# Group normalization in place: 32 written-out tiles become a loop of 8 iterations over 4 fixed buffers

## The chip, the cores and the metric

The kernel runs on one core of a Trainium2 chip. The metric is the device time of one execution in microseconds (us); less is better. The core has five engines that work side by side: TensorE (PE), VectorE (DVE), ScalarE (ACT), GpSimd (POOL) and SyncE (SP). Transfers between memory (HBM) and the on-chip buffers are carried by sixteen DMA engines; an engine such as SP only issues them, in the order of its own instruction stream, and an issue that has to wait on a semaphore holds up everything behind it on that engine.

## The reference

The input `x` is bf16 of shape (128, 1024, 32, 16): 134.2 MB in and as much out. For each of the 128 samples the 1024 channels form 32 groups of 32 channels. Each group is normalized with its own mean and variance, then scaled and shifted by channel:

```python
    xr = x.reshape(B, G, C // G, H, W)
    mu = xr.mean(axis=(2, 3, 4), keepdims=True)
    var = ((xr - mu) ** 2).mean(axis=(2, 3, 4), keepdims=True)
    xn = (xr - mu) / jnp.sqrt(var + 1e-5)
    xn = xn.reshape(B, C, H, W)
    return xn * g[None, :, None, None] + b[None, :, None, None]
```

## The kernel before

One tile holds 4 samples: the 128 partitions are 4 samples by 32 groups, and each partition holds one group of 32 channels by 512 positions, 16,384 bf16 values. A tile is 4 MB, loaded with one DMA and stored with one DMA, and there are `NT` = 32 of them. A tile is normalized in place: the store reads the buffer that the load filled.

Work on a tile `i`, in order:

- `sums` (line 130): PE adds up the tile, 32 matmuls of 512 columns with an identity matrix, accumulated in one PSUM tile `ps`.
- `squares` (lines 148 and 161): ACT takes a rough shift `nshift` from the first 512 values, then sums the squares of the shifted values in four parts of 4096.
- `moments` (lines 180 to 213): DVE reduces `ps` to the negative mean, and with the shift and the four sums of squares gets the variance (`jv`, line 213).
- `root` (line 231): ACT takes the square root. `apply` (lines 241 to 264): DVE takes the reciprocal, forms scale and offset by channel (`scl`, `bia`), and applies them with 32 instructions of 512 values each.
- `store(i)` (line 78), and then `load(i + 5)` (line 74) into the buffer of tile `i - 1`. Both are issued by SP.

The loop over the tiles is a Python loop, so the program is written out: all 32 tiles stand one behind the other in each engine's instruction stream. The helper `chain` fixes the order of each engine's instructions as they are written. `XBUFS` = 6 buffers are loaded ahead of the loop. The scale and the offset (`g` and `b`, 2 KB each, needed by all four samples) are fetched with eight small DMAs issued by ACT. DMAs share eight completion semaphores in turn; one that takes a semaphore again waits until its former DMA has landed.

Of the kernel before, what the change touches and what calls it, by code (L numbers as in the profile page):

```python
# [10 lines left out]
F32 = mybir.dt.float32  # L11
BF16 = mybir.dt.bfloat16
# [1 line left out]
NUM_GROUPS = 32  # L14
EPS = 1e-5

XBUFS = 6
MM_FREE = 512
SQ_PARTS = 4

# [2 lines left out]
def kernel(  # L23
# [8 lines left out]
    nc = tc.nc  # L32
    P = nc.NUM_PARTITIONS
    B0, C, H, W = x.shape
    G = NUM_GROUPS
# [3 lines left out]
    NT = B0 // NS  # L39
    F = KC * HW  # L40
# [4 lines left out]
    x_v = x.rearrange("(t n) (q k) h w -> t (n q) (k h w)", n=NS, q=G)  # L45
    o_v = out.rearrange("(t n) (q k) h w -> t (n q) (k h w)", n=NS, q=G)
    g_v = g.rearrange("(q k) -> q k", q=G)
    b_v = b.rearrange("(q k) -> q k", q=G)

    consts = ctx.enter_context(tc.tile_pool(name="consts", bufs=1))  # L50
    xpool = ctx.enter_context(tc.tile_pool(name="xpool", bufs=XBUFS))
    jpool = ctx.enter_context(tc.tile_pool(name="jpool", bufs=1))
    spool = ctx.enter_context(tc.tile_pool(name="spool", bufs=4))
    pspool = ctx.enter_context(
        tc.tile_pool(name="pspool", bufs=3, space=bass.MemoryType.PSUM)
    )

    last = {}
# [4 lines left out]
    def chain(key, inst):  # L63
        prev = last.get(key)
        if prev is not None:
            tc.add_manual_dep(inst.ins, prev.ins.name, nosync, reason="engine order")
        last[key] = inst
        return inst

    state = {}  # L70

    def load(i):
        xt = xpool.tile([P, F], BF16, name="xt")
        chain("sp", nc.sync.dma_start(out=xt[:], in_=x_v[i]))  # L74
        state[i] = {"xt": xt}

    def store(i):
        chain("sp", nc.sync.dma_start(out=o_v[i], in_=state[i]["xt"][:]))
        state.pop(i)

    for i in range(XBUFS):
        load(i)

    gam_b = consts.tile([P, KC], BF16)
    bet_b = consts.tile([P, KC], BF16)
    for n in range(NS):
        chain("act", nc.scalar.dma_start(out=gam_b[n * G : (n + 1) * G, :], in_=g_v))
        chain("act", nc.scalar.dma_start(out=bet_b[n * G : (n + 1) * G, :], in_=b_v))

    eps_t = consts.tile([P, 1], F32)  # L90
    nc.vector.memset(eps_t[:], EPS)  # L91
# [7 lines left out]
        out=half[:],  # L99
        in_=ones[:],  # L100
# [6 lines left out]
    eye = consts.tile([P, P], BF16)  # L107
    nc.gpsimd.affine_select(  # L108
        out=eye[:],
        in_=half[:],  # L110
# [9 lines left out]
    chain("dve", nc.vector.tensor_copy(out=gam[:], in_=gam_b[:]))  # L120
    chain("dve", nc.vector.tensor_copy(out=bet[:], in_=bet_b[:]))

    def sums(i):

        st = state[i]
        ps = pspool.tile([P, MM_FREE], F32, name="ps")
        for k in range(NMM):
            chain(
                "pe",
                nc.tensor.matmul(  # L130
                    out=ps[:],
                    lhsT=eye[:],
                    rhs=st["xt"][:, k * MM_FREE : (k + 1) * MM_FREE],
                    start=(k == 0),
                    stop=(k == NMM - 1),
                ),
            )
        st["ps"] = ps

    def squares(i):  # L140

        st = state[i]
        xt = st["xt"]
        nshift = spool.tile([P, 1], F32, name="nshift")
        ja = jpool.tile([P, SQ], BF16, name="ja")
        chain(
            "act",
            nc.scalar.activation(  # L148
                out=ja[:, 0:HW],
                in_=xt[:, 0:HW],  # L150
                func=ACT.Identity,
                scale=-1.0 / HW,
                accum_out=nshift[:],
            ),
        )
        sq = spool.tile([P, SQ_PARTS], F32, name="sq")
        for k in range(SQ_PARTS):
            ja = jpool.tile([P, SQ], BF16, name="ja")
            chain(
                "act",  # L160
                nc.scalar.activation(  # L161
                    out=ja[:],
                    in_=xt[:, k * SQ : (k + 1) * SQ],
                    func=ACT.Square,
                    bias=nshift[:],
                    scale=1.0,
                    accum_out=sq[:, k : k + 1],
                ),
            )
        st["nshift"] = nshift  # L170
        st["sq"] = sq

    def moments(i):

        st = state[i]
        negmean = spool.tile([P, 1], F32, name="negmean")
        jd = jpool.tile([P, MM_FREE], BF16, name="jd")
        chain(
            "dve",
            nc.vector.tensor_scalar(  # L180
                out=jd[:],
                in0=st["ps"][:],
                scalar1=-inv_n,
                scalar2=None,
                op0=ALU.mult,
                op1=ALU.add,
                accum_out=negmean[:],
            ),
        )
        d = spool.tile([P, 1], F32, name="d")  # L190
        chain(
            "dve",
            nc.vector.tensor_tensor(  # L193
                out=d[:], in0=negmean[:], in1=st["nshift"][:], op=ALU.subtract
            ),
        )
        nd2 = spool.tile([P, 1], F32, name="nd2")
        chain(
            "dve",
            nc.vector.tensor_scalar(  # L200
                out=nd2[:],
                in0=d[:],
                scalar1=d[:],
                scalar2=-1.0,
                op0=ALU.mult,
                op1=ALU.mult,
            ),
        )
        var = spool.tile([P, 1], F32, name="var")
        jv = spool.tile([P, SQ_PARTS], F32, name="jv")  # L210
        chain(
            "dve",
            nc.vector.tensor_scalar(  # L213
                out=jv[:],
                in0=st["sq"][:],
                scalar1=inv_n,
                scalar2=nd2[:],
                op0=ALU.mult,
                op1=ALU.add,
                accum_out=var[:],  # L220
            ),
        )
        st["negmean"] = negmean
        st["var"] = var

    def root(i):
        st = state[i]
        rstd = spool.tile([P, 1], F32, name="rstd")
        chain(
            "act",  # L230
            nc.scalar.activation(  # L231
                out=rstd[:], in_=st["var"][:], func=ACT.Sqrt, bias=eps_t[:], scale=1.0
            ),
        )
        st["rstd"] = rstd

    def apply(i):
        st = state[i]
        rstd = st["rstd"]
        xt = st["xt"]  # L240
        chain("dve", nc.vector.reciprocal(out=rstd[:], in_=rstd[:]))  # L241
        scl = spool.tile([P, KC], F32, name="scl")
        bia = spool.tile([P, KC], F32, name="bia")
        chain(
            "dve",
            nc.vector.tensor_scalar(  # L246
                out=scl[:], in0=gam[:], scalar1=rstd[:], scalar2=None, op0=ALU.mult
            ),
        )
        chain(  # L250
            "dve",
            nc.vector.scalar_tensor_tensor(  # L252
                out=bia[:],
                in0=scl[:],
                scalar=st["negmean"][:],
                in1=bet[:],
                op0=ALU.mult,
                op1=ALU.add,
            ),
        )  # L260
        for k in range(KC):
            chain(
                "dve",
                nc.vector.tensor_scalar(  # L264
                    out=xt[:, k * HW : (k + 1) * HW],
                    in0=xt[:, k * HW : (k + 1) * HW],
                    scalar1=scl[:, k : k + 1],
                    scalar2=bia[:, k : k + 1],
                    op0=ALU.mult,
                    op1=ALU.add,  # L270
                ),
            )

    for i in range(NT):
        sums(i)
        squares(i)
        moments(i)
        root(i)
        apply(i)
        store(i)  # L280
        if i >= 1 and i + XBUFS - 1 < NT:
            load(i + XBUFS - 1)


# [28 lines left out]
```

## Time and profile before

| | |
|---|---|
| Median of 3 runs | 639.44 us (638.84 to 639.48) |
| Time of the profiled execution | 638.97 us |
| Its span in the profile | 637.3 us |
| DMA | 268.71 MB, mean 422 GB/s; the load and store queue q1 takes 98.2% of 16 engines' span |
| Busy share of the span | ACT 82%, DVE 62%, PE 45% |
| One tile on ACT | 4 x 3708 ns of squares, 624 ns for the shift, 5 x about 186 ns of accumulator reads, 294 ns for the root |
| One tile of `apply` on DVE | 32 x 404 ns mean, starts about 0.33 us apart: 10.4 us |

The profiled execution's time is 1.67 us more than its span, which runs from the first to the last instruction. The page cuts the span into 40 slices of 15.9 us; a digit is a busy share in tenths, and 9 means 90% or more. In the chain of work that ended last each piece has its start, its length and what it was; a DMA's piece runs from its issue to its landing, so the time that it spends queued behind older transfers is part of it. In a list of waits each line names who waited, for whom, the total, the number of times and the longest wait; "SPq" is SP's issuing queue.

### The profile page before, as it was taken

Reading aid. Unit: us, or ns where it says so; the run is one execution under the profiler, and the core shown is the slowest. Engines: PE = TensorE matmul, PEld = TensorE weight load, DVE = VectorE, ACT = ScalarE, POOL = GpSimd, SP = SyncE. Lnnn points to the kernel's source line nnn. Section 1 sums busy time; section 2 is a strip of 40 time slices with the busy share of each in tenths; the row PEclk is TensorE's granted clock in tenths of the full one; section 3 lists DMA queues with packets and bytes.
Section 4 is the critical chain, followed back from the end, with each engine's and each line's share of the span. In section 5 each row is a group of like instructions: output and inputs, shape, how many; then the busy total and the mean of one; then the engine's idle time right before and its main releaser. Section 6 shows DMA issues by size and latency. Waiting matters only on the chain.

```text
span 637.3 us, 3988 instructions
## 1 busy us (share of the span) xinstructions
PE 289.4 (45%) x1004; PEld 113.9 (18%) x1024; DVE 395.7 (62%) x1316; ACT 519.5 (82%) x354; POOL 0.8 (0%) x6
## 2 busy tenths in 40 slices
PE   1868505544355542556334654335652356533400
PEld 0323202211122211222111221112220122211100
DVE  0277777777777755577655676555765557755560
ACT  2999999999999887988788978879887898788800
POOL 0000000000000000000000000000000000000000
PEclk9899857656877567876678766787666877667755
DMA  7999999999999999999999999999999999999993
GB/s 301 438 436 403 430 437 433 428 430 428 430 438 430 434 426 432 427 440 426 436 434 431 428 438 432 432 427 438 430 429 435 435 430 432 430 432 433 436 430 171
DMA packets 9623, 268.71 MB, mean 422 GB/s; under 512 B 1408, under 2 KB 1408, under 8 KB 1408
## 3 DMA queue, kind: packets, MB, share of 16 engines
q1 hardware_dynamic: 9216, 268.44, 98.2%
q8 instruction: 8, 0.13, 0.1%
q14 instruction: 15, 0.12, 0.0%
q10 hardware_dynamic: 384, 0.02, 0.0%
HBM read 134.23 MB, written 134.22 MB: 421 GB/s over the span
## 4 chain that ended last, share of the span: by engine, by line
DMA 73%; ACT 13%; PE 6%; DVE 4%; issue 0%; SPq 0%; DVEq 0%; ACTq 0%
DMA out_dram<-xt 48%; DMA xt<-in_x_dram 25%; ACT ja L161 12%; PE ps L130 6%; DVE xt L264 3%; ACT ja L148 1%; DVE jd L180 0%; SPq L74 0%; DVE jv L213 0%; ACT rstd L231 0%; DVE bia L252 0%; DVE scl L246 0%; DVE rstd L241 0%; DVEq L308 0%; DVE nd L200 0%
## 5 line engine op out<-in xcount | busy, mean ns | idle before, releaser
L161 ACT ACTIVATE ja<-xt,nshift 128x4096 bf16<-128x4096 bf16 x128 | 474.6, 3708 | 4.1
L130 PE MATMUL ps<-xt,eye 128*128 128x512 bf16 x1004 | 289.4, 455 | 307.5 <-DMA xt<-in_x_dram 281.2
L264 DVE TENSOR_SCALAR xt<-xt,scl,bia 128x512 bf16<-128x512 bf16 x1024 | 333.6, 404 | 1.2
L130 PEld LDWEIGHTS <-eye 128*128 128x128 bf16 x1024 | 113.9, 114 | 482.5 <-DMA xt<-in_x_dram 303.0
L213 DVE TENSOR_SCALAR_CACHE_REDUCE jv<-sq,nd 128x4 f32<-128x4 f32 x32 | 6.9, 217 | 157.4 <-ACT ja L161 157.4
L148 ACT ACTIVATE ja<-xt 128x512 bf16<-128x512 bf16 x32 | 20.0, 624 | 63.8 <-DMA xt<-in_x_dram 63.8
L180 DVE TENSOR_SCALAR_CACHE_REDUCE jd<-ps 128x512 bf16<-128x512 f32 x32 | 22.0, 688 | 28.8 <-PE ps L130 27.3
L161 ACT ACTIVATION_READ_ACCUMULATOR ja<-xt,nshift 128x1 f32 x128 | 23.9, 186 | 0.0
L231 ACT ACTIVATE rstd<-var,eps_t 128x1 f32<-128x1 f32 x32 | 9.4, 294 | 9.4 <-DVE jv L213 9.4
L241 DVE RECIPROCAL rstd<-rstd 128x1 f32<-128x1 f32 x32 | 5.2, 164 | 11.6 <-ACT rstd L231 11.6
L252 DVE SCALAR_TENSOR_TENSOR bia<-scl,negmean,bet 128x32 f32<-128x32 f32 x32 | 8.0, 251 | 1.1
L246 DVE TENSOR_SCALAR scl<-gam,rstd 128x32 f32<-128x32 f32 x32 | 7.7, 242 | 1.1
L120 DVE CAST gam<-gam_b 128x32 f32<-128x32 bf16 x1 | 0.2, 181 | 12.9 <-DMA bet_b<-in_b_dram 12.9
L200 DVE TENSOR_SCALAR nd<-d 128x1 f32<-128x1 f32 x32 | 6.9, 214 | 1.1
L93 ACT ACT_TABLE_LOAD x1 | 1.3, 1283 | 7.3 <-DMA gam_b<-in_g_dram 7.3
L193 DVE TENSOR_TENSOR d<-negmean,nshift 128x1 f32<-128x1 f32 x32 | 5.1, 159 | 3.3
L148 ACT ACTIVATION_READ_ACCUMULATOR ja<-xt 128x1 f32 x32 | 6.0, 187 | 0.0
L213 DVE DVE_READ_ACCUMULATOR jv<-sq,nd 128x1 f32 x32 | 2.6, 83 | 0.0
L180 DVE DVE_READ_ACCUMULATOR jd<-ps 128x1 f32 x32 | 2.6, 82 | 0.0
L91 DVE MEMSET eps_t<- 128x1 f32 x1 | 0.1, 59 | 0.9 <-PEq L297 0.9
L98 POOL TENSOR_SCALAR_AFFINE_SELECT half<-ones 128x128 bf16<-128x128 bf16 x1 | 0.3, 295 | 0.7 <-DVE ones L96 0.7
L108 POOL TENSOR_SCALAR_AFFINE_SELECT eye<-half 128x128 bf16<-128x128 bf16 x1 | 0.3, 294 | 0.1
(7 smaller groups left out, 0.9 us busy)
## 6 DMA issues: line engine op xcount, KB each, us to landing
xt<-in_x_dram SPq DMA_DIRECT2D x32, 4096.0 KB, 29.0
out_dram<-xt SPq DMA_DIRECT2D x32, 4096.0 KB, 39.1
gam_b<-in_g_dram ACTq DMA_DIRECT2D x4, 2.0 KB, 10.3
bet_b<-in_b_dram ACTq DMA_DIRECT2D x4, 2.0 KB, 9.8
```

Of the source, the lines that this page charges most:

```text
L130: nc.tensor.matmul(out=ps[:], lhsT=eye[:], rhs=st["xt"][:, k * MM_FREE : (k + 1) * MM_FREE], start=(k == 0), stop=(k == NMM - 1),),
L148: nc.scalar.activation(out=ja[:, 0:HW], in_=xt[:, 0:HW], func=ACT.Identity, scale=-1.0 / HW, accum_out=nshift[:],),
L161: nc.scalar.activation(out=ja[:], in_=xt[:, k * SQ : (k + 1) * SQ], func=ACT.Square, bias=nshift[:], scale=1.0, accum_out=sq[:, k : k + 1],),
L180: nc.vector.tensor_scalar(out=jd[:], in0=st["ps"][:], scalar1=-inv_n, scalar2=None, op0=ALU.mult, op1=ALU.add, accum_out=negmean[:],),
L193: nc.vector.tensor_tensor(out=d[:], in0=negmean[:], in1=st["nshift"][:], op=ALU.subtract),
L200: nc.vector.tensor_scalar(out=nd2[:], in0=d[:], scalar1=d[:], scalar2=-1.0, op0=ALU.mult, op1=ALU.mult,),
L213: nc.vector.tensor_scalar(out=jv[:], in0=st["sq"][:], scalar1=inv_n, scalar2=nd2[:], op0=ALU.mult, op1=ALU.add, accum_out=var[:],),
L231: nc.scalar.activation(out=rstd[:], in_=st["var"][:], func=ACT.Sqrt, bias=eps_t[:], scale=1.0),
L241: chain("dve", nc.vector.reciprocal(out=rstd[:], in_=rstd[:]))
L246: nc.vector.tensor_scalar(out=scl[:], in0=gam[:], scalar1=rstd[:], scalar2=None, op0=ALU.mult),
L252: nc.vector.scalar_tensor_tensor(out=bia[:], in0=scl[:], scalar=st["negmean"][:], in1=bet[:], op0=ALU.mult, op1=ALU.add,),
L264: nc.vector.tensor_scalar(out=xt[:, k * HW : (k + 1) * HW], in0=xt[:, k * HW : (k + 1) * HW], scalar1=scl[:, k : k + 1], scalar2=bia[:, k ...
```

## The change

The 32 tiles become a hardware loop of 8 iterations, each of which works through 4 tiles. The buffers are four fixed tiles `x0` to `x3`. Across iterations, waits compare semaphores with registers that grow from one iteration to the next (`iteration_sync="reg_based"`). The addresses of loads and stores come from the loop variable. Three loads stand ahead of the loop, not six; in the loop, tile `i` is followed by `store(i)` and the load of tile `i + 3`. In the last iteration the loads past the end carry a condition that skips them. Stores are declared not to depend on each other. The scale and offset loads move from ACT to SP, between loads 0 and 1. Each tile gets two small new instructions, a one-column matmul into `pt` on PE and a one-column copy into `jt` on ACT, which read the tile before the large ones do.

```diff
-XBUFS = 6
+XBUFS = 4
...
-    xpool = ctx.enter_context(tc.tile_pool(name="xpool", bufs=XBUFS))
+    xpool = ctx.enter_context(tc.tile_pool(name="xpool", bufs=1))
...
+    ptpool = ctx.enter_context(
+        tc.tile_pool(name="ptpool", bufs=1, space=bass.MemoryType.PSUM)
     )
...
-    def load(i):
-        xt = xpool.tile([P, F], BF16, name="xt")
-        chain("sp", nc.sync.dma_start(out=xt[:], in_=x_v[i]))
-        state[i] = {"xt": xt}
-
-    def store(i):
-        chain("sp", nc.sync.dma_start(out=o_v[i], in_=state[i]["xt"][:]))
-        state.pop(i)
-
-    for i in range(XBUFS):
-        load(i)
+    bufs = [xpool.tile([P, F], BF16, name=f"x{j}") for j in range(XBUFS)]
+
+    def load(j, i, cond=None):
+        chain("sp", nc.sync.dma_start(out=bufs[j][:], in_=x_v[i], cond=cond))
+
+    def store(j, i):
+
+        st = chain("sp", nc.sync.dma_start(out=o_v[i], in_=bufs[j][:]))
+        tc.declare_no_dep(st.ins, group="stores", across_iterations=True, reason="rows of its own")
+        tc.add_to_no_dep_group("stores", st.ins)
+
+    load(0, 0)
...
-        chain("act", nc.scalar.dma_start(out=gam_b[n * G : (n + 1) * G, :], in_=g_v))
-        chain("act", nc.scalar.dma_start(out=bet_b[n * G : (n + 1) * G, :], in_=b_v))
+        chain("sp", nc.sync.dma_start(out=gam_b[n * G : (n + 1) * G, :], in_=g_v))
+        chain("sp", nc.sync.dma_start(out=bet_b[n * G : (n + 1) * G, :], in_=b_v))
+
+    for j in range(1, XBUFS - 1):
+        load(j, j)
...
+        pt = ptpool.tile([P, 1], F32, name="pt")
+        chain(
+            "pe",
+            nc.tensor.matmul(
+                out=pt[:], lhsT=eye[:], rhs=st["xt"][:, 0:1], start=True, stop=True
+            ),
+        )
...
+        jt = jpool.tile([P, 1], BF16, name="jt")
+        chain("act", nc.scalar.copy(out=jt[:], in_=xt[:, 0:1]))
...
-    for i in range(NT):
-        sums(i)
-        squares(i)
-        moments(i)
-        root(i)
-        apply(i)
-        store(i)
-        if i >= 1 and i + XBUFS - 1 < NT:
-            load(i + XBUFS - 1)
+    def compute(j):
+        st = {"xt": bufs[j]}
+        sums(st)
+        squares(st)
+        moments(st)
+        root(st)
+        apply(st)
+
+    with tc.For_i(0, NT, XBUFS, iteration_sync="reg_based") as t:
+        last.clear()
+        for j in range(XBUFS):
+            compute(j)
+            store(j, t + j)
+            n = XBUFS - 1 + j
+            load(n % XBUFS, t + n if j == 0 else (t + n) % NT, None if j == 0 else t < NT - XBUFS)
```

More of the change, by code (lines that the diff above doesn't have):

```diff
@@ L68, in chain @@
         return inst
-    state = {}
-    def load(i):
-        xt = xpool.tile([P, F], BF16, name="xt")
-        chain("sp", nc.sync.dma_start(out=xt[:], in_=x_v[i]))
-        state[i] = {"xt": xt}
-    def store(i):
-        chain("sp", nc.sync.dma_start(out=o_v[i], in_=state[i]["xt"][:]))
-        state.pop(i)
-    for i in range(XBUFS):
-        load(i)
+    bufs = [xpool.tile([P, F], BF16, name=f"x{j}") for j in range(XBUFS)]
[6 more added lines that the diff above has]
+    load(0, 0)
     gam_b = consts.tile([P, KC], BF16)
@@ L121, with sums @@
     chain("dve", nc.vector.tensor_copy(out=bet[:], in_=bet_b[:]))
-    def sums(i):
-        st = state[i]
+    def sums(st):
+        pt = ptpool.tile([P, 1], F32, name="pt")
[4 more added lines that the diff above has]
+            ),
+        )
         ps = pspool.tile([P, MM_FREE], F32, name="ps")
@@ L138, in sums, with squares @@
         st["ps"] = ps
-    def squares(i):
-        st = state[i]
+    def squares(st):
         xt = st["xt"]
+        jt = jpool.tile([P, 1], BF16, name="jt")
+        chain("act", nc.scalar.copy(out=jt[:], in_=xt[:, 0:1]))
         nshift = spool.tile([P, 1], F32, name="nshift")
@@ L171, in squares, with moments @@
         st["sq"] = sq
-    def moments(i):
-        st = state[i]
+    def moments(st):
         negmean = spool.tile([P, 1], F32, name="negmean")
@@ L224, in moments, with root @@
         st["var"] = var
-    def root(i):
-        st = state[i]
+    def root(st):
         rstd = spool.tile([P, 1], F32, name="rstd")
@@ L235, in root, with apply @@
         st["rstd"] = rstd
-    def apply(i):
-        st = state[i]
+    def apply(st):
         rstd = st["rstd"]
```

## The prediction

> **What bounds the kernel now.** I began with the engine totals and the 40 slices of the page.
>
> ```profile
> PE 289.4 (45%) x1004; PEld 113.9 (18%) x1024; DVE 395.7 (62%) x1316; ACT 519.5 (82%) x354; POOL 0.8 (0%) x6
> ...
> DMA  7999999999999999999999999999999999999993
> GB/s 301 438 436 403 430 437 433 428 430 428 430 438 430 434 426 432 427 440 426 436 434 431 428 438 432 432 427 438 430 429 435 435 430 432 430 432 433 436 430 171
> ```
>
> No compute engine is full (ACT leads with 82%), but the DMA row reads 9 from the second slice to the last but one. The sixteen DMA engines set the time, and only the first and last slices show them short of work. Next, the chain that ended last, where it stands on transfers.
>
> ```profile
> 0.80 12.25 DMA xt<-in_x_dram
> ...
> 126.36 38.82 DMA out_dram<-xt
> ...
> 165.64 39.23 DMA out_dram<-xt
> ...
> 519.18 39.09 DMA out_dram<-xt
> ...
> 558.35 28.97 DMA xt<-in_x_dram
> ```
>
> A load into an idle queue takes 12.25 us (the first; it lands at 13.05). In the stream a store takes 39 us because three transfers stand before it. The store issued at 126.36 is tile 5's and lands at 165.18; the one issued at 519.18 is tile 25's and lands at 558.27. So 20 tiles take 393.09 us: **19.65 us for one load and one store**, 9.83 us each. The last load lands at 587.32. Then SP's timeline and its waits.
>
> ```profile
> 40.97 0.35 SPq L78 DMA_DIRECT2D out_dram<-xt  x1
> ```
>
> ```profile
> 615.29 0.33 SPq L78 DMA_DIRECT2D out_dram<-xt  x1
> ```
>
> ```profile
> SPq L74 <- DMA out_dram<-xt: 472.4, 26, 19.5
> SPq L78 <- DVE xt L264: 100.1, 7, 25.4
> SPq L74 <- DMA xt<-in_x_dram: 11.9, 1, 11.9
> ```
>
> Tile 0's store goes out at 40.97, 27.92 us after its load landed; the last at 615.29, 27.97 us after its own. That 28 us is the **tile latency**: ACT's squares, the moments, then 32 DVE applications. SP's 26 long waits are loads that wait until an older store has emptied a buffer; the wait of 11.9 us shows that already now the second load goes out only after the first has landed. The DMA view of the last 23 us gives the last store's time:
>
> ```profile
> out_dram<-xt SPq DMA_DIRECT2D x1, 4096.0 KB, 21.1
> ```
>
> It lands at 636.4, and 0.9 us later the span ends (637.3). It was issued 21 us ahead, so it still queued behind older stores: neither the first nor the last tile's latency is exposed today.
>
> **The change, part by part.** *Scale and offset loads on SP.* Eight issues stand on SP between loads 0 and 1, and in the built program the last of them waits for load 0, as load 1 does now. Seven issues at about 0.45 us (from ACT's timeline, 0.42 to 0.69) fit in the 11.9 us that SP waits there; the eighth puts loads 1 and 2 0.5 us later, nothing to the end, since ACT reaches tile 1 only 16.5 us after tile 0. ACT loses its eight issues and its 7.3 us before the table load, worth nothing: it waits for load 0 anyway.
>
> *Three loads ahead instead of six, and load 3 behind store 0.* This decides the start. In SP's new order load 3 stands behind store 0, although its buffer is empty, and store 0 waits for the tile latency. Tile latency grows by ACT's touch copy (128x1; the rows of that size on ACT are 0.20 and 0.29 us) and some register instructions, unshown; the 0.02 us pieces between instructions on the chain bound them at some 0.1 us together, one 0.4 us DMA issue from above. I take 0.3: 28.3 us. Load 2 lands at 13.05 + 0.5 + 12.3 + 9.7 = 35.6 and the queue runs dry. Store 0 goes out at 13.05 + 28.3 = 41.4 and, from an idle queue, lands 12.3 us later: 53.7. An idle store is not in the trace; 12.25 is the idle load's row, and 9.7 (no start-up at all) and 15 bound it. The order is then load 3, store 1, load 4, ..., so tile 4's store is the twelfth transfer and lands at 53.7 + 8 x 9.83 = 132.3. The twelfth transfer before is tile 3's store, which the chain lands at 125.9. **Start: +6.4 us.**
>
> *The middle.* A tile's store follows its load in the queue after four others (39.3 us). It needs the tile latency (28.3) and must be issued 2.6 us early (12.3 - 9.7): 8.4 us to spare. ACT needs 16.5 us a tile beside 19.65. Each load waits for the store before last, as now, and goes out as that lands, two transfers ahead of its turn. So four buffers still keep the queue full; the copy, PE's extra 1-column matmul (at most 0.46 + 0.11 us; PE idles 10 us a tile) and register waits lie under the 8.4 us. Dynamic addresses may add a fraction of a 0.4 us issue on SP, hidden by its long waits. A late back edge is hidden too: behind a waiting SP stand the next store and load, and both have this reserve. I take **0** for the seven back edges; bounds are -0.3 us a tile (clean pairs at 19.36, from neighbouring loads' landings; say -8 in all) and +2 us an iteration (+14).
>
> *The end.* Load 31 lands last among the loads, after store 28, as transfer 61: 53.7 + 57 x 9.83 = 614.0. Only stores 29 and 30 follow, 19.7 us of work, and then the queue is dry until store 31 goes out at 614.0 + 28.3 = 642.3, landing 12.3 later at 654.6. Before, transfer 61 landed three transfers before 636.4, near 607.2. So after transfer 61 it now takes 40.6 us, not 29.2: **end +11.4 us**. Three loads are skipped; their waits (the store before last) stand on SP ahead of stores 30 and 31, but stores 28 and 29 land before the data of 30 and 31 are ready. Loop exit adds a barrier: 0.5 taken, 0 to 3 us. The span ends at 654.6 + 0.9 + 0.5 = **656.0**.
>
> The sum is against the profiled execution: span 637.3, time 638.97, thus 1.67 outside the span; the median of the three runs is 0.47 higher. 656.0 + 1.67 + 0.47 = 658.1.
>
> The Trainium skill, in DMA: Bandwidth & Descriptors, section Anatomy of one DMA, gives a transfer as 2.0 us plus its bytes over 436 GB/s. By it an idle 4 MB transfer would be estimated at 11.6 us, not 12.25, and the sum 1.3 us lower. I keep the row.
>
> **The rivals.** *Back edges cost the stream.* The unrolled program fetches its instructions in order:
>
> ```profile
> q8 instruction: 8, 0.13, 0.1%
> q14 instruction: 15, 0.12, 0.0%
> ```
>
> That is 8 fetches of 16 KB and 15 of 8 KB. The loop could refetch its body each time (DVE's is 205 instructions, PE's 277), and either stall an engine or take DMA time. The q8 row's 0.1% of 16 engines' span is some 10 us, about 1.3 us a fetch; two more such on one DMA engine per iteration give 2 to 3 us x 7, near 672. For it: one late DMA engine holds up every landing. Against: an engine's stall has 8.4 us of cover, and ACT's 2.7 us idle a tile absorbs it. The Trainium skill, Runtime: NRT & Kernel Launch, section Instruction fetch mechanics, speaks for this rival: prefetch is sequential and a taken branch out of a two-page window stalls for a fetch. By that rule each engine would stop at each back edge, and by its 16 KB pages a DVE body of 205 could stay inside; the trace's second queue shows 8 KB pieces, not 16. No run here yet shows a back edge.
>
> *Four buffers are too few.* If latency plus issue exceeds 39.3 us, every tile pays. With 2 us over, 28 x 2 = 56: near 714; 0.5 us over, near 672. It needs 8.4 us that I can't name.
>
> *The waits don't overlap iterations.* If growing registers act as a drain, each of seven back edges exposes about 40.6 - 29.5 + 6.4 = 17.5 us: near 781. The waits in the built program compare with counts that the previous iteration has reached long before, so this is weak. So is the skip that does not skip: three loads, +10 us to +29.
>
> *A cleaner stream* (a small form of the next): landings 9.68 us apart without the fetches between, -8: 650.
>
> *Other side: a stream fast enough to pay for both ends.* Fewer transfers in flight and fewer fetches could speed up the pairs. Price: 28 pairs x the gain; it decides from 18.7 / 28 = 0.67 us a pair, that is 18.98 us, or 442 GB/s. Then 639.4, and less beyond. For it: some slices reach 438 to 440. Against: no full slice passes 440, and the clean pairs stop at 19.36.
>
> **How the numbers follow.** Forecast, both ends exposed and a full stream: 0.62. Cleaner stream, 650: 0.14. Back edges, 672: 0.12. Too few buffers: 0.05. Drains or unskipped loads: 0.04. Other side: 0.03, of it 0.01 within the 0.2% that a measurement of this kernel can tell from no change. The predicted time is the likeliest case's, 658. The range is 647 to 672: from the cleaner stream with a quick idle store (2.5 us less) to the back edges. Faster 0.02, same 0.01, slower 0.97.
>
> **What would show it.** Right: the DMA row falls in the third slice (near 36 to 44 us) and again near the end; the first store issues near 41 and lands near 54; steady pairs 19.65 us apart; the last load lands near 614 and the last store, issued 28 us later, takes about 12 us instead of 21. Wrong: pairs further apart or dips at every fourth tile (back edges), no dip at the start (load 3 got ahead of store 0), or a store issued late against its turn in the middle.

## The result, and the profile after

The changed kernel takes 663.53 us (median of 4 runs, 663.13 to 664.49) and the kernel before 639.27 us beside it (638.84 to 639.48): a ratio of 1.0383, 95% interval 1.0365 to 1.0401. The change costs some 24 us; 19 were predicted. The profiled execution took 663.21 us with a span of 661.2.

The page of the changed kernel: busy time of the engines, the DMA engines' share in 40 slices (16.5 us each), and the two queues.

```profile
PE 293.0 (44%) x1040; PEld 116.2 (18%) x1056; DVE 396.4 (60%) x1316; ACT 523.5 (79%) x386; POOL 0.8 (0%) x6
...
DMA  7949999999999999999999999999999999999555
GB/s 288 442 191 381 444 420 434 438 426 428 434 430 430 430 426 434 432 422 440 436 422 440 434 424 438 436 424 440 432 418 436 420 416 422 434 424 430 230 256 254
...
q1 hardware_dynamic: 9600, 268.46, 95.2%
q14 instruction: 2, 0.02, 0.0%
```

The compute engines do the same work as before. The two places where the DMA row falls are the two of the prediction: the third slice (4; 191 GB/s) and now the last three (5 5 5). Between them it is all 9: the loop leaves no dip at any fourth tile. The row of the 16 KB instruction fetches (q8) is gone, and q14 holds 2 fetches where the written-out kernel had 15.

SP's timeline at the start and at the end (start, length, instruction):

```profile
13.23 0.31 SPq L91 DMA_DIRECT2D bet_b<-in_b_dram  x1
13.58 0.91 SPq L77 DMA_DIRECT2D x<-in_x_dram  x2
...
43.09 0.36 SPq L81 DMA_DIRECT2D out_dram<-x  x1
43.80 0.36 SPq L77 DMA_DIRECT2D x<-in_x_dram  x1
...
628.37 0.36 SPq L81 DMA_DIRECT2D out_dram<-x  x1
...
647.91 0.36 SPq L81 DMA_DIRECT2D out_dram<-x  x1
648.78 0.08 SPq L77 DMA_DIRECT2D x<-in_x_dram  x1
```

Load 3 stands behind store 0, and nothing is issued between 14.5 and 43.1 us while loads 1 and 2 land at 25.88 and 35.59: the queue is dry for 7.5 us. At the end a skipped load costs SP 0.08 us, and store 31 goes out into an idle queue.

The chain that ended last, in order of time; a DMA's piece runs from issue to landing:

```profile
0.81 12.40 DMA x<-in_x_dram
13.23 1.48 DMA bet_b<-in_b_dram
...
331.60 21.62 DMA out_dram<-x
...
568.83 21.62 DMA out_dram<-x
590.60 29.31 DMA x<-in_x_dram
```

A store now lands 21.6 us after its issue, not 39: fewer transfers stand before it. Tile 15's store lands at 353.22 and tile 27's at 590.45, so 12 tiles take 237.23 us, **19.77 us a tile** (19.65 before). The last load lands at 619.91, 28.0 us before store 31 goes out. The second piece was not expected on this chain: a load of 2 KB stands between load 0 and the first work on it.

The prediction's points against the trace, with the written-out twin of the first experiment in the last column (us from the start of the span):

| | before | predicted | after | twin |
|---|---|---|---|---|
| tile 0 starts on ACT | 13.08 | 13.1 | 14.95 | 13.13 |
| store 0 issued | 40.97 | 41.4 | 43.09 | 41.12 |
| store 0 lands (after its issue) | 76.67 | 53.7 (12.3) | 55.18 (12.1) | 53.22 (12.1) |
| steady pairs | 19.65 | 19.65 | 19.77 | 19.65 |
| load 31 lands | 587.3 | 614.0 | 619.9 | 616.1 |
| store 31 issued | 615.3 | 642.3 | 647.9 | 644.1 |
| store 31 lands (after its issue) | 636.4 (21.1) | 654.6 (12.3) | 659.0 (11.1) | 655.2 (11.1) |
| span ends | 637.3 | 656.0 | 661.2 | 656.0 |

### The profile page after: what moved, and what is told of

Read it like the earlier page. It is cut to its first block, busy times and chain, and to the rows that moved or that the text cites. A ratio compares the mean times of both kernels' runs of the same rounds, so it can differ in the third digit from the quotient of the medians.

```text
span 661.2 us, 5054 instructions
## 1 busy us (share of the span) xinstructions
PE 293.0 (44%) x1040; PEld 116.2 (18%) x1056; DVE 396.4 (60%) x1316; ACT 523.5 (79%) x386; POOL 0.8 (0%) x6
## 3 DMA queue, kind: packets, MB, share of 16 engines
q1 hardware_dynamic: 9600, 268.46, 95.2%
## 4 chain that ended last, share of the span: by engine, by line
DMA 59%; issue 23%; DVE 13%; ACT 2%; DVEq 0%; SPq 0%; ACTq 0%
DMA x<-in_x_dram 36%; DMA out_dram<-x 23%; DVE x L274 12%; ACT ja L174 1%; ACT ja L161 0%; ACT rstd L242 0%; DVE bia L262 0%; DVE scl L256 0%; DMA bet_b<-in_b_dram 0%; DVE rstd L251 0%; DVE jv L225 0%; ACT jt L156 0%; DVEq L292 0%; SPq L77 0%; DVEq L324 0%
## 5 line engine op out<-in xcount | busy, mean ns | idle before, releaser
L174 ACT ACTIVATE ja<-x,nshift 128x4096 bf16<-128x4096 bf16 x128 | 474.6, 3708 | 4.1
L274 DVE TENSOR_SCALAR x<-x,scl,bia 128x512 bf16<-128x512 bf16 x1024 | 333.6, 405 | 2.1
L142 PE MATMUL ps<-x,eye 128*128 128x512 bf16 x1008 | 290.5, 456 | 2.2 <-issue 1.8
L134 PE MATMUL pt<-x,eye 128*128 128x1 bf16 x32 | 5.5, 173 | 334.4 <-DMA x<-in_x_dram 246.7
L142 PEld LDWEIGHTS <-eye 128*128 128x128 bf16 x1024 | 114.2, 114 | 168.0 <-issue 92.7
L156 ACT COPY jt<-x 128x1 bf16<-128x1 bf16 x32 | 6.2, 193 | 98.9 <-DMA x<-in_x_dram 83.4
L134 PEld LDWEIGHTS <-eye 128*128 128x128 bf16 x32 | 3.3, 104 | 344.9 <-DMA x<-in_x_dram 153.5
L174 ACT ACTIVATION_READ_ACCUMULATOR ja<-x,nshift 128x1 f32 x128 | 23.8, 186 | 0.0
L161 ACT ACTIVATE ja<-x 128x512 bf16<-128x512 bf16 x32 | 20.1, 628 | 0.0
L251 DVE RECIPROCAL rstd<-rstd 128x1 f32<-128x1 f32 x32 | 5.2, 164 | 11.6 <-ACT rstd L242 11.6
L161 ACT ACTIVATION_READ_ACCUMULATOR ja<-x 128x1 f32 x32 | 6.0, 186 | 0.0
```

The source lines that it names most:

```text
L134: nc.tensor.matmul(out=pt[:], lhsT=eye[:], rhs=st["xt"][:, 0:1], start=True, stop=True),
L142: nc.tensor.matmul(out=ps[:], lhsT=eye[:], rhs=st["xt"][:, k * MM_FREE : (k + 1) * MM_FREE], start=(k == 0), stop=(k == NMM - 1),),
L156: chain("act", nc.scalar.copy(out=jt[:], in_=xt[:, 0:1]))
L161: nc.scalar.activation(out=ja[:, 0:HW], in_=xt[:, 0:HW], func=ACT.Identity, scale=-1.0 / HW, accum_out=nshift[:],),
L174: nc.scalar.activation(out=ja[:], in_=xt[:, k * SQ : (k + 1) * SQ], func=ACT.Square, bias=nshift[:], scale=1.0, accum_out=sq[:, k : k + 1],),
L274: nc.vector.tensor_scalar(out=xt[:, k * HW : (k + 1) * HW], in0=xt[:, k * HW : (k + 1) * HW], scalar1=scl[:, k : k + 1], scalar2=bia[:, k ...
```

## The experiments

The theory after the first result: both ends cost what the prediction says, and the 5 us more come from the loop itself, at its entry, through the small loads, and at its exit. Its rivals: the loop slows the transfers in the middle (register addresses, conditions, back edges), or the four buffers do; then a written-out kernel of the same order would be at the predicted 658 only by accident.

### Is it the loop, or the order and the four buffers?

**twin_unrolled**: the changed kernel's order, buffers and small instructions, written out.

```diff
-    with tc.For_i(0, NT, XBUFS, iteration_sync="reg_based") as t:
...
+    for i in range(NT):
+        compute(i % XBUFS)
+        store(i % XBUFS, i)
+        n = i + XBUFS - 1
+        if n < NT:
+            load(n % XBUFS, n)
```

> The changed kernel written out: four fixed buffers, three loads ahead, store i then load i+3, parameter loads on SP, touch instructions, but a Python loop instead of the hardware loop. Theory 1 (the order of the transfers costs, not the loop): near the changed kernel, 660 to 664 us, with the same dry queue near 36 to 43 us and the last store issued about 28 us after the last load lands. Within it, two small terms of the loop should move: tile 0 starts near 13.2 us instead of 14.9, because no engine waits for another to enter a loop (-1.7 us), and load-store pairs are 19.65 us as in the kernel before (instruction fetches come back) or stay 19.77 (then it is the four buffers). Theory 2 (the back edges and register waits cost): at or below 645 us.

Measured: 658.18 us (657.73 to 658.55), ratio 1.0301 [1.0284, 1.0318], span 656.0, somewhat below the expected times. So about 19 us come from order and depth, and the loop itself costs 5.3 us. The table's last two columns say where: 2.0 at store 0, 1.8 in the stream, 1.4 between the last landing and the end of the span (2.2 against 0.8). The page of the twin has both dips without any loop:

```profile
DMA  7959999999999999999999999999999999999665
```

That the twin's span is the predicted 656.0 to the tenth is luck: its stream from store 0 to load 31 is 2.6 us longer than the sum had it (562.9, not 560.3), and its other terms are 2.6 us shorter together.

**before_4_buffers**: the kernel before with `XBUFS` = 4 (not 6); its own order keeps load 3 ahead of store 0.

> The kernel before with 4 buffers instead of 6: written out, its own order and parameter loads, four loads ahead. Theory 1: both ends are exposed, a little less at the start than in the changed kernel: 652 to 656 us, last store issued 28 us after the last load landed and taking 11 to 12 us instead of 21. Rival (four buffers are enough, the loop costs): 639 to 641 us.

Measured: 654.58 us (654.47 to 654.72), 1.0243 [1.0226, 1.026], as expected. Its steady pairs are 19.67: four buffers keep the queue full in the middle. The cost is at the ends: its last load lands at 612.87, and nothing covers the last tile. From its chain that ended last:

```profile
583.89 28.98 DMA xt<-in_x_dram
```

The three runs take the change apart: of the 24 us, some 15.5 come with four buffers, another 3.6 with the rest of the twin (load 3 behind store 0, the small loads on SP, the small instructions), and 5.3 with the loop.

**before_5_buffers**: the same with `XBUFS` = 5.

> The kernel before with 5 buffers instead of 6. With 4 it took 654.6. Theory 1 (the ends are exposed only where less than the tile latency of 28 us is queued behind the last load): the last load is then followed by three other stores (29 us) before the last one, just enough, and five loads (51 us) cover the first 41 us: 639 to 640 us, no different from 6 buffers. Rival (each buffer less costs its share): half of the way to 4 buffers, 646 to 647.

Measured: 639.49 us (638.98 to 640.22), 1.0007 [0.9997, 1.0016]: no difference from six. Each buffer less moves the last load later (587.3, 598.2, 612.9), and one tile of 28.0 us and one idle store of 11.1, 39.1 us together, are a floor under the end behind it. With four buffers the last store lands on that floor (651.93). With five the floor is at 637.3, and the last store lands at 637.67, 9.65 us behind the one before it, as in a full stream; the stream of the six-buffer kernel runs out at 636.43. Five is where the floor meets the stream.

### Load 3 behind store 0

**loop_load3_ahead**: load 3 goes ahead of the loop, and its place in the first iteration is skipped.

```diff
-    for j in range(1, XBUFS - 1):
+    for j in range(1, XBUFS):
...
-            load(n % XBUFS, t + n if j == 0 else (t + n) % NT, None if j == 0 else t < NT - XBUFS)
+            load(n % XBUFS, t + n if j == 0 else (t + n) % NT, t > 0 if j == 0 else t < NT - XBUFS)
```

> The changed kernel with load 3 put ahead of the loop (and skipped in the first iteration), so that it no longer stands behind store 0. Theory 1: the dry queue before store 0 is filled by load 3, but a shorter one opens behind store 0, since load 4 stands behind store 1, which waits for tile 1 (issue near 59.7): in all 3 us less, 660 to 661 us. Rival (the start is hidden work, only the end costs): no change, 663.5. Rival (the whole gap of the start is load 3's place): 7 us less, 656.5.

Measured: 660.67 us (659.84 to 661.24), 1.0335 [1.0318, 1.0352], 2.9 us less than the changed kernel and as expected. The dip gets shallower (247 GB/s in its lowest early slice, not 191) and the last load lands at 617.65, not 619.91. It does not vanish: the queue is now dry behind store 0, which lands at 55.56, until store 1 goes out at 60.11, and load 4 stands behind that store.

### The 1.9 us at which tile 0 starts later

The profile of the changed kernel names the loop's own line (292) as what tile 0 waits for. From its list of waits (who, for whom: total, times, longest):

```profile
DVE gam L126 <- DMA gam_b<-in_g_dram: 13.4, 1, 13.4
ACT jt L156 <- SPq L292: 12.6, 1, 12.6
```

At the entry to the loop PE, ACT, SP and DVE each signal the others (PE and ACT by 1.0 us, SP and DVE only from 14.5 to 15.1), and the first reads of load 0, on PE and ACT, wait for SP's and DVE's signals. DVE enters only after its two casts; these wait for the eight small loads. Seven of them, issued from 1.26 to 4.12 us, land only behind load 0, from 13.38 to 14.40; the eighth, which takes over load 0's completion semaphore, is issued at 13.23 and lands at 14.71. The timeline shows them in line:

```profile
14.52 0.18 DVE L126 CAST gam<-gam_b 128x32 f32<-128x32 bf16 x1 [13.40 <-DMA gam_b<-in_g_dram]
14.73 0.18 DVE L127 CAST bet<-bet_b 128x32 f32<-128x32 bf16 x1
14.95 0.19 ACT L156 COPY jt<-x 128x1 bf16<-128x1 bf16 x1 [12.64 <-SPq L292]
```

In the twin ACT does not wait for the casts:

```profile
13.13 0.19 ACT L156 COPY jt<-x 128x1 bf16<-128x1 bf16 x1 [10.83 <-DMA x<-in_x_dram]
14.39 0.18 DVE L126 CAST gam<-gam_b 128x32 f32<-128x32 bf16 x1 [13.29 <-DMA gam_b<-in_g_dram]
```

Two experiments moved the eight loads, in the loop kernel, to **loop_params_act** and **loop_params_pool**:

```diff
-        chain("sp", nc.sync.dma_start(out=gam_b[n * G : (n + 1) * G, :], in_=g_v))
+        chain("act", nc.scalar.dma_start(out=gam_b[n * G : (n + 1) * G, :], in_=g_v))
```

(the second with `chain("pool", nc.gpsimd.dma_start(...))`; both move the `bet_b` loads likewise).

> The changed kernel with the scale and offset loads back on ACT. The loop starts an engine's work on tile 0 only when SP and DVE have set the semaphores that they own at the loop's entry. Theory 1a (DVE's entry holds tile 0): the last small load still waits for load 0, DVE still casts after it, tile 0 still starts near 14.9: 663 to 664 us, although loads 1 and 2 go out near 7 us instead of 13.6. Theory 1b (only SP's eight issues hold tile 0): SP enters early, tile 0 starts near 13.2, 661.5 to 662 us.

Measured: 663.32 us (663.05 to 664.58), 1.0389 [1.0372, 1.0406]: no gain. Loads 1 and 2 go out at 13.23 and 13.62, not near 7 as expected; SP still enters the loop some 0.4 us earlier. But the last small load, though issued at 7.06, lands at 14.31, again behind load 0, and ACT's wait is now put down to DVE:

```profile
14.68 0.19 ACT L156 COPY jt<-x 128x1 bf16<-128x1 bf16 x1 [5.78 <-DVEq L292]
```

> The changed kernel with the scale and offset loads on GpSimd's queue, so that neither SP nor DVE waits for load 0 ahead of the loop. Theory 1 (a or b): tile 0 starts near 13.2 us instead of 14.9 and store 0 goes out near 41.3 instead of 43.1: 661.5 to 662 us. Rival (tile 0's late start comes from the loop's branch and first fetch, not from the small loads): 663.5.

Measured: 672.89 us (672.38 to 673.51), 1.0529 [1.0512, 1.0547]: 9.4 us slower than the changed kernel where a gain was expected. It shows the mechanism by its opposite. With nothing between loads 0 and 1, SP issues all three large loads by 2.2 us; the small loads on GpSimd then share the sixteen engines with 12 MB, and land one after the other from 8.35 to 23.96. The list of waits, and the page's slices:

```profile
ACT jt L156 <- DVEq L292: 22.0, 1, 22.0
DVE gam L126 <- DMA gam_b<-in_g_dram: 21.5, 1, 21.5
```

```profile
DMA  9808999999999999999999999999999999999655
```

Load 0 has landed at 13.43, but ACT waits until 24.3 for DVE's entry, and PE until 24.2. Store 0 goes out at 52.63, 9.5 us later than in the changed kernel, and the total takes over all of it. So PE and ACT pay at the loop's entry for what makes DVE late.

**before_params_sp** and **before_params_pool** make the same moves in the kernel before.

> The kernel before with the scale and offset loads moved to SP between loads 0 and 1, nothing else. Theory 1: no change, 639 to 640 us (load 1 goes out 0.5 us later and the stream starts that much later). Rival (the move holds up the stream): 642 us or more.

Measured: 639.11 us (638.98 to 639.45), 1.0002 [0.9992, 1.0011]: the move that the change makes costs nothing without the loop, as its term in the prediction had it.

> The kernel before with the scale and offset loads on GpSimd's queue. Load 1 then shares no semaphore with load 0's wait and goes out right behind it, so the 2.4 us pause of the stream at 13 us goes: 636.5 to 637 us, faster than both kernels. Rival (the pause is made up later): 639.

Measured: 636.53 us (636.05 to 636.96), 0.9961 [0.9947, 0.9975]: **faster than both kernels**, by 2.4 us against the kernel before in the same set of runs (638.90). SP's timeline shows six loads issued without a pause, where the kernel before waited for load 0 after the first:

```profile
0.81 3.02 SPq L74 DMA_DIRECT2D xt<-in_x_dram  x6
```

Its small loads are as late as in the loop: DVE's timeline has the casts 8 to 9 us later than in the kernel before (14.05 and 14.24).

```profile
21.93 0.18 DVE L120 CAST gam<-gam_b 128x32 f32<-128x32 bf16 x1 [20.82 <-DMA gam_b<-in_g_dram]
23.39 0.18 DVE L121 CAST bet<-bet_b 128x32 f32<-128x32 bf16 x1 [1.28 <-DMA bet_b<-in_b_dram]
23.48 0.68 DVE L180 TENSOR_SCALAR_CACHE_REDUCE jd<-ps 128x512 bf16<-128x512 f32 x1
```

But without a loop only DVE waits for them, and its next work, the reduction of PE's sums, came at 23.10 in the kernel before and comes at 23.48 now: they are hidden. The same edit gains 2.4 us in one kernel and costs 9.4 in the other.

### Does the loop slow the stream?

In the trace's landings the loop alternates 9.69 us (load) and 10.08 us (store), from the third iteration on in all alike. The written-out kernels land every 9.68 us, with one step of 10.49 in six. That step comes with an 8 KB instruction fetch: in the kernel before the fetches at 353.69, 412.59 and 471.48 are followed by the long steps to 362.22, 421.11 and 480.01. So a pair takes (5 x 9.68 + 10.49) / 3 = 19.63. So the loop did gain what the prediction's cleaner stream asked for, no fetches, and lost it, and 0.12 us more, to slower stores. Three edits looked for the reason.

**loop_fixed_store_rows**: the store's row no longer comes from a register. The kernel writes the rows of tiles 0 to 3 in every iteration and leaves out the others.

```diff
-            store(j, t + j)
+            store(j, j)
```

> The changed kernel, but the stores of all iterations write the rows of tiles 0 to 3 (the other rows of the output are left out), so that a store's address needs no register. Every store in the loop takes 10.07 us in the stream, against 9.68 in the written-out twin. Theory 3 (the register address makes the store slower): stores at 9.68, pairs at 19.37 to 19.4, about 28 x 0.38 = 10.6 us less: 653 us. Rival (something else in the loop): 10.07 again, 663.5 us.

Measured: 662.97 us (662.61 to 663.3), 1.0376 [1.0359, 1.0393]; stores still 10.07. The store's register address is not the reason.

**loop_loads_not_skipped**: the loads past the end have no condition, and load tiles again.

```diff
-            load(n % XBUFS, t + n if j == 0 else (t + n) % NT, None if j == 0 else t < NT - XBUFS)
+            load(n % XBUFS, t + n if j == 0 else (t + n) % NT, None)
```

> The changed kernel without the conditions: the three loads past the end are carried out (they read tiles 0 to 2 again, into buffers whose stores have landed; the output stays). It prices the rival that the skip does not skip, and asks whether the condition makes the stores of the loop 10.07 us long. Theory 1: after load 31 the stream has three stores and three loads, 59 us, where it now has 39 us: 20 us more, 683 us. Stores stay at 10.07 us in the stream if the condition is not their cause, and go to 9.68 (10 us less, 673) if it is.

Measured: 682.7 us (682.43 to 683.25), 1.0685 [1.0667, 1.0703], as expected. The skip works and is worth 19 us: q1 moves 281.04 MB here and 268.46 in the changed kernel. Landings still alternate 9.69 and 10.08, so the condition is not the reason either. SP's waits show what the skip saves (292 is the loop's line; SP waits there for the last landings):

```profile
SPq L292 <- DMA x<-in_x_dram: 18.4, 2, 9.6
```

**loop_8_tiles**: 4 iterations of 8 tiles, the same order of work.

```diff
-    with tc.For_i(0, NT, XBUFS, iteration_sync="reg_based") as t:
+    STEP = 2 * XBUFS
+    with tc.For_i(0, NT, STEP, iteration_sync="reg_based") as t:
...
+        for u in range(STEP):
+            compute(u % XBUFS)
+            store(u % XBUFS, t + u)
```

> The changed kernel with 8 tiles in the loop's body and 4 iterations. The bodies grow to 405 instructions on DVE and 554 on PE, from 205 and 277, whose loop fetched no instruction between its first and last iteration. Theory 1: four back edges less change nothing (each lies under a reserve of 8 us): 663 to 664 us. If the body of 405 no longer stays in the engine's instruction memory, fetches return in the list of queues, a few tenths of a us each for the stream: up to 665. Rival (a back edge costs, 0.3 to 0.4 us of it visible on SP): 662. Rival (a taken branch to an instruction that has to be fetched stalls the engines beyond the reserve): 670 or more.

Measured: 664.88 us (664.21 to 665.6), 1.0407 [1.039, 1.0424]. Half the back edges give the same stream (pairs 19.76) and no gain in all: the profiled span is 1.0 us shorter (660.2), and the time outside the span 4.0 us instead of 2.0. Its trace has two 8 KB instruction fetches behind the span's end, at 661.18 and 663.79, where the changed kernel has none; whether they are what the extra time goes to, no run here shows.

What the slower stores are can be seen at the end of the stream. The DMA view of the changed kernel from 620 to 661 us, in 40 slices of 1.03 us:

```profile
GB/s 192 160 32 64 32 32 32 0 32 512 512 512 512 480 224 320 512 512 0 0 0 0 0 0 0 0 0 0 512 512 512 512 512 0 512 512 512 0 0 8
```

512 is all sixteen engines with a packet of 32 KB, and 32 is one. Load 31 has landed (619.9), store 29 has been in the queue since 608.59, and yet it lands only at 629.99: all but three engines are through with it by 623, and from 624.7 to 629.2 **one** engine moves its share alone. The sixteen are not in step. Each takes its share of every transfer in order, a landing is that of the last, and one engine has fallen behind by about a transfer in the course of the run: the sixteen completion marks of load 1 come within 0.6 us (25.32 to 25.88), those of load 31 within 9.7 (610.22 to 619.91). The trace's packet records show its steps: in the loop, eight packets in a row of a store take longer than the 1213 ns of the others (from 303.1 to 313.2 us 1236 to 1298 ns, 10.09 us in sum, the store's spacing). In the twin such packets take 1218 to 1265 ns and a row of them near 9.9 us, so there the lag that comes with the fetches (0.8 us every three tiles, 0.27 a tile) is the larger and sets the pace. The sixteen engines have work nearly all the time in between, which is why the DMA row reads 9 throughout. The kernel before ends the same way; its DMA view from 606 to 637 us, in slices of 0.78 us, where one engine is 42:

```profile
GB/s 423 423 465 423 423 507 423 338 507 423 381 465 296 592 381 296 634 423 296 592 381 381 507 254 592 254 211 211 85 169 85 0 85 0 42 42 0 42 0 0
```

From 626 on ever fewer engines have work, and the last 3.9 us (632.2 to 636.1) belong to one. Why the slow engine's store packets take longer in the loop than in the twin stays open: the register address, the condition and the number of back edges are excluded, and no run here separates what is left.

### Can smaller stores give the ends back?

**loop_quarter_stores**: each store in four parts of 1 MB, each of which can go out as soon as its 8 applications are done.

```diff
+        for h in range(SPLIT):
+            w = slice(h * F // SPLIT, (h + 1) * F // SPLIT)
+            st = chain("sp", nc.sync.dma_start(out=o_v[i][:, w], in_=bufs[j][:, w]))
```

> The changed kernel with each store split into four DMAs of 1 MB, each of which goes out as soon as its eight channels are done. Theory 1: the first quarter of a tile goes out 7.8 us before its last, so the dry queue before store 0 shrinks from 8.7 to about 1 us, and after the last apply only 1 MB is left: about 7 us less at the start and 7 at the end, 648 to 651 us. Rival (the gaps are not what sets the time): 663. Rival (96 more transfers cost the stream their own start): 663 to 675.

Measured: 662.78 us (658.48 to 664.82), 1.0381 [1.0361, 1.0402]: almost nothing of the gain that was expected. The profiled execution is the fastest of the four (658.48 us, span 656.8; the others took 662.0 to 664.8), so it shows the best case. In it both ends did gain: store 0 has landed at 47.76 instead of 55.18, and the last part of store 31 lands 31.9 us after load 31 instead of 39.1. But load 31 lands at 623.05 instead of 619.91. From store 0 to load 31 the stream takes 575.3 us, not 564.7: 10.6 us are given back, 0.4 a tile. Two things show. Load 3 still stands behind the last part of store 0 (issued at 43.72, as before), so the early start brings no load forward. And with four stores a tile the eight completion semaphores come round again within two tiles, so that a store waits for a load of the tile before to land. SP's waits and its timeline:

```profile
SPq L84 <- DMA x<-in_x_dram: 65.2, 7, 10.0
```

```profile
103.37 16.09 SPq L84 DMA_DIRECT2D out_dram<-x  x4
```

The fourth of those stores goes out at 119.13, just after the load that held its semaphore lands (119.01), and its load behind it goes out late too; about one tile in four has its load land 20.8 to 21.0 us after the former instead of 19.9. Seven such steps, each some 1.1 us above the 19.77 of the changed kernel, are 7.9 of the 10.6; the rest is left to the smaller transfers, which no run here takes apart.

## Why the prediction was right, and where it was off

**Start, +6.4: right in its cause, 1.7 too small at store 0.** The queue runs dry behind store 0 as told, and the idle store takes 12.1 us (12.3 taken). The Trainium skill's 11.6 us for such a transfer (DMA: Bandwidth & Descriptors, section Anatomy of one DMA, an estimate from a fit to transfers that GpSimd issues, while SP issues these) lies between this row and the 11.1 us of the last store; neither would have changed the reading. What was missed stands in the term "Tile latency grows by ... 0.3": the tile latency did not grow (28.0 at the end), but tile 0 itself started 1.87 us later. The step "Seven issues ... fit in the 11.9 us that SP waits there; the eighth puts loads 1 and 2 0.5 us later, nothing to the end" asked only what SP's queue holds up. It did not ask who waits for the small loads once a loop begins: DVE, and through the entry PE and ACT. By tile 4's store, where the prediction closes this part, the miss is 2.7 (135.03, not 132.3); the difference belongs to the stream and stands in the next part.

**Middle, 0 with bounds -8 and +14: 4.4 too small.** The sum's 57 x 9.83 = 560.3 us from store 0 to load 31 were 564.7. The steady pairs make up 28 x 0.12 = 3.4 of the difference; the other 1.0 lies in the restart after the dry queue, where load 3 lands 10.7 us and store 1 another 10.0 us later, not 9.83 each. The price of 19.65 was taken from a stream that carried instruction fetches, and both parts of it changed at once: the fetches went (as the cleaner stream said), the stores slowed.

**End, +11.4: right.** Load 31 to store 31 is 28.0 us (28.3), its landing another 11.1 (12.3): 1.5 quicker together. The loop's exit takes 2.2 us to the end of the span, not 1.4, within the 0 to 3 given for the barrier; an 8 KB instruction fetch at 660.2 falls into it.

In all, the loop itself was priced at 0.5 (its exit) and cost 5.2 of the span beside its twin. The sum of the misses: 1.7 - 0.2 + 4.4 - 0.3 - 1.2 + 0.8 = 5.2 us, which is 661.2 - 656.0.

**The rivals.** *Back edges* did not fetch: between 35 and 660 us the trace has not one instruction fetch, and no slice dips. The rule of the Trainium skill (Runtime: NRT & Kernel Launch, section Instruction fetch mechanics) that a taken branch stalls where its target is out of a two-page window did not bite here, as it would not if the whole body stayed inside the window; a body of 8 tiles was still not refetched, and a longer one was not tried. On SP the branch and its register work take some 0.5 us (95.9 to 96.4 at the end of the first iteration), under its waits. *Four buffers too few* fell for the middle, as the 8.4 us of reserve said, and is the whole story of the end. *Drains* fell: no slice dips between the two ends. *The skip that doesn't skip* fell: the run without the condition pays 19 us. *A cleaner stream* was half right. *The other side* fell: the pairs got slower, and no run's steady pairs came below those of the kernel before (19.63 in the middle of its stream).

## What to carry to other kernels

When a stream of transfers is the bound, the buffer count is decided at the ends, not in the middle: here the last load must land 39.1 us (one tile's latency and one idle store) before the stream runs out; five buffers just do that, and four lack 15 us. Write down the order on the issuing queue for the first few tiles, since a load whose buffer is free but which stands behind a store costs its wait. And treat the entry of such a loop as a meeting of the engines: here what DVE's prologue waited for, 2 KB of constants, delayed the first tile on PE and ACT, while the same loads cost nothing in the written-out program.

## What was not expected of the hardware

- The sixteen DMA engines drift apart within a saturated stream and a landing waits for the last of them: in both kernels one engine is left alone at the end of the stream, for 4.5 us (624.7 to 629.2) in the changed kernel and for 3.9 (632.2 to 636.1) in the kernel before. The Trainium skill notes two engines as usually slower in traces (DMA: Bandwidth & Descriptors, section Latency and other measured facts) and ties its guess to the descriptors of transfers issued from GpSimd; here GpSimd issues none, and the trace does not number the engines.
- A loop of 4 or 8 tiles fetches no instructions between its first and its last iterations (2 and 4 fetches within the span, 23 in the written-out twin).
- 2 KB loads that shared the engines with queued 4 MB loads took 7 to 19 us each, growing in the order of their issue: the eight, issued from 1.33 to 4.89 us, landed from 8.35 to 23.96.
